# One order of work for five engines, made anew: an adaLN transformer block with sliding-window attention on one core

## The chip, the cores and the metric

The kernel runs on one core of a Trainium2 chip. The core has a matrix engine (TensorE, PE in the profile; its weight loads are listed as PEld), three engines for elementwise work (VectorE or DVE, ScalarE or ACT, GpSimd or POOL), and SyncE (SP), which here does nothing but issue transfers. Each engine runs its own list of instructions in order and waits on semaphores for the others. Sixteen DMA engines move the data of all queues. The metric is the device time of one execution in microseconds (us); a lower time is better.

## What is computed

One input `x` of 2048 rows and 640 columns in bf16, six modulation vectors made from a conditioning row `c`, and two sub-blocks with a residual each:

```python
sa, ca, ga, sb, cb, gb = six rows of (silu(c) @ w_mod)
h = layernorm(x) * (1 + ca) + sa
x = x + ga * A(h)          # 32 heads of 20 columns, causal, window of 256 keys, softmax, @ wo
h = layernorm(x) * (1 + cb) + sb
x = x + gb * B(h)          # (sigmoid(h @ w_gate) * (h @ w_up)) @ w_down, hidden 1536
```

## The kernel before

The 2048 rows are cut into eight chunks of 256 rows, numbered 0 to 7 below (two blocks of 128 rows each). Per chunk the work goes through these stages; the name in brackets is the builder's tag, and the line is the one that the profile shows.

- The chunk of `x` is loaded ("x0" to "x7", L521/L524). VectorE takes the statistics (four `bn_stats`, L732; two `bn_aggr`, L734), GpSimd makes the inverse deviation (L738, L740), and the normalised rows are written (L753 on VectorE, L750 on GpSimd).
- They are turned so that columns lie on partitions. Chunks 0 and 1 are turned on TensorE. From chunk 2 on a DMA transpose does it ("atr", L760, `hT<-x`), and five instructions per chunk apply scale and shift afterwards ("amodu", L768/L769, on any of three engines).
- TensorE projects queries, keys and values in halves of 320 columns (L625, `M<-wq,hT` and so on); VectorE or ScalarE copies each half from PSUM (L655/L656, "evqk", "evv"). Queries and keys go to a staging buffer `stg`, of which there are two, and from chunk 1 on four DMA transposes per chunk turn them, one block of queries or keys each ("qkt", L760, `QT<-stg`, `KT<-stg`). The next chunk's projection may write `stg` only when these transposes have landed.
- Attention: a set of eight or sixteen score matmuls fills the one score tile `S` (L626), ScalarE takes the exponential of all of it (L975, 90 times in the kernel), GpSimd masks it (L983/L985). The product with the values (L626, `M<-E,V`) comes once per half of the heads and fills two PSUM banks, which VectorE transposes (L1021) before they are free again; the result is normalised, turned and projected with `wo` (L625), and VectorE adds the residual (L1094).
- The second norm and its DMA transpose ("btr", `h2T<-x`) follow, then the gated MLP (L625, L1138, L1140) and the output.

PSUM has four banks for everything but the scores (`M`), given out one by one.

The order is not found while building. `Prog.op` notes every operation with what it reads and writes. `Prog.schedule` then goes through the list `PLAN`, which has one number per operation: the number divided by five is the operation in the order of its making, the rest says which engine takes it (0 PE, 1 ACT, 2 DVE, 3 POOL, 4 SP). The place in the list is thus the place in that engine's queue. `SLOTS` gives the buffer of each tile in the same order. `emit` (L279) adds a semaphore wait wherever an operation depends on another engine's, on a landing, or on the last users of its buffer; a transfer carries one of 24 semaphores in turn and also waits for the transfer that had it last. Two more rules touch the steps below: a GpSimd operation waits for the latest VectorE operation that is marked `port`, and `x5` may be loaded only when the transpose of chunk 3 (number 1499) has landed, because it takes that chunk's buffer:

```python
raw = src = load_x(p_x0, a, 0.55 if a < 4 else 20 + 0.1 * a, eng=XE, extra=turned[a - 2])
```

A transfer that waits holds up all that stand behind it in SP's queue; an instruction that waits on VectorE, ScalarE or GpSimd holds up its engine.

Of the kernel before, what the change touches and what calls it, by code (L numbers as in the profile page):

```python
# [305 lines left out]
def c_pe(n):  # L306
# [4 lines left out]
    76, 68, 139, 89, 228, 3, 8, 53, 43, 63, 33, 13, 175, 84, 202, 182, 186, 192, 197, 94, 99, 104, 342, 337, 752, 347,  # L311
    205, 210, 215, 230, 220, 732, 327, 322, 109, 28, 48, 114, 363, 368, 124, 377, 332, 425, 235, 240, 245, 250, 435,
    353, 119, 747, 737, 742, 757, 358, 372, 134, 57, 72, 763, 768, 772, 431, 380, 255, 386, 441, 260, 777, 265, 270,
    275, 390, 820, 280, 287, 457, 447, 467, 462, 451, 780, 406, 396, 402, 129, 585, 423, 827, 590, 485, 417, 597, 786,
    411, 1149, 570, 575, 470, 581, 475, 490, 497, 535, 600, 482, 540, 606, 546, 144, 520, 525, 531, 510, 500, 635, 550,
    506, 556, 1152, 517, 640, 790, 620, 646, 1525, 1167, 1157, 1172, 625, 1162, 1177, 797, 632, 700, 705, 1531, 670,
    610, 810, 675, 1439, 38, 617, 682, 711, 1540, 816, 650, 800, 1546, 685, 690, 1457, 807, 657, 1462, 1447, 18, 164,
    1183, 1538, 1188, 696, 1193, 23, 890, 715, 720, 1198, 1467, 1202, 1555, 726, 560, 660, 895, 905, 910, 567, 1442,
    1561, 875, 880, 1595, 666, 901, 154, 294, 149, 1601, 1452, 917, 1553, 1209, 860, 865, 830, 845, 1473, 850, 856,
    1478, 1568, 835, 1610, 887, 959, 1608, 872, 842, 964, 1616, 1216, 954, 1570, 1030, 935, 1212, 1227, 1582, 1577,  # L320
    1233, 1623, 1223, 1483, 1037, 1625, 1587, 1057, 920, 925, 932, 1631, 1492, 940, 970, 1000, 975, 1592, 2635, 946,
    981, 1040, 1005, 1047, 1012, 1638, 1052, 969, 159, 1265, 1270, 2641, 985, 990, 1107, 1277, 1097, 1102, 2655, 996,
    1640, 1647, 1652, 2544, 1420, 1015, 1425, 1020, 2661, 2675, 1235, 1240, 1325, 1488, 2653, 1027, 1431, 2681, 1280,
    1250, 1087, 1657, 1330, 1092, 2695, 1662, 1079, 174, 1074, 314, 1499, 1336, 2701, 2668, 1247, 1285, 1310, 1315,
    1295, 1300, 1667, 1672, 1322, 2715, 1306, 1061, 1255, 1675, 1690, 1680, 2721, 2552, 1262, 2562, 319, 1695, 1405,
    2547, 1687, 1292, 2567, 1702, 169, 1359, 1364, 2735, 1720, 1725, 1705, 1710, 1717, 2557, 2741, 1375, 1410, 2688,
    2755, 1506, 2761, 2713, 2693, 1390, 2673, 2708, 2733, 1395, 1521, 1511, 1501, 2648, 2728, 2753, 2748, 3099, 1069,
    1732, 1369, 2572, 1417, 1402, 2578, 1380, 1742, 1340, 1345, 2583, 1518, 2588, 2598, 1752, 1757, 1737, 1352, 1374,
    2775, 1747, 1386, 2802, 1762, 2781, 2593, 2603, 2768, 2415, 1110, 2340, 2420, 2788, 1768, 1773, 2773, 2815, 3122,
    3117, 2609, 2797, 2427, 2345, 2821, 2355, 1137, 1117, 2793, 3102, 2352, 1777, 2360, 2400, 2495, 2405, 2366, 2835,  # L330
    2510, 2411, 1782, 2632, 2430, 2385, 2500, 2515, 2507, 2390, 304, 299, 2464, 2841, 2626, 2522, 2828, 2855, 2861,
    2397, 2618, 2469, 2853, 2613, 2370, 2435, 2445, 2480, 2450, 1789, 2375, 2622, 2441, 2875, 2457, 2833, 2873, 2848,
    2485, 2479, 1824, 2955, 2881, 2382, 2474, 2970, 2960, 2807, 3107, 2492, 2868, 2910, 1141, 2975, 3127, 2967, 2893,
    2888, 3190, 1120, 2982, 1132, 3196, 2915, 2895, 2525, 2530, 2900, 3112, 2922, 1127, 2907, 2812, 1792, 3210, 2985,
    3237, 1813, 3133, 1796, 2536, 1801, 3208, 3138, 3143, 3153, 3216, 1829, 3019, 309, 3232, 1834, 1084, 4269, 1807,
    3242, 1852, 2990, 1895, 3080, 3085, 2925, 2930, 2996, 3091, 1857, 3247, 1867, 2937, 3845, 3148, 3158, 3851, 1920,
    1925, 1900, 1930, 1905, 1910, 2940, 1915, 1935, 1819, 1940, 3865, 2945, 3257, 3252, 1946, 2952, 1952, 1955, 1960,
    1965, 1980, 1970, 1975, 1985, 1990, 1995, 3260, 2000, 3871, 3885, 3863, 3164, 3858, 1883, 3878, 3223, 2006, 3265,
    3272, 2012, 3035, 3275, 3280, 2040, 2045, 3040, 3047, 3891, 3905, 1837, 2050, 3000, 3005, 2015, 2020, 2055, 3029,
    3903, 3911, 3188, 3918, 3898, 3883, 3012, 2025, 2030, 2035, 2066, 3065, 3070, 3077, 2060, 3925, 3287, 3034, 3290,  # L340
    3024, 5429, 3228, 3923, 3203, 3181, 3931, 2072, 4287, 3295, 2100, 2105, 2075, 2080, 2085, 2110, 3322, 3302, 4292,
    3327, 2115, 2120, 2090, 1842, 1847, 2095, 2126, 2135, 2140, 2145, 2150, 2155, 2132, 1887, 3945, 2186, 3951, 2160,
    2165, 1873, 1863, 1893, 2170, 2175, 4277, 2180, 3967, 3972, 5447, 2192, 3332, 2195, 3050, 3305, 3310, 3985, 3991,
    3055, 2220, 2225, 2230, 2200, 3062, 2205, 2210, 2215, 3958, 3963, 1877, 3317, 2246, 3337, 3342, 3347, 5432, 2315,
    4005, 4011, 3176, 2255, 2260, 2235, 2320, 2240, 5437, 4003, 4025, 2252, 2295, 2300, 2265, 3938, 3168, 2305, 4031,
    3353, 3358, 3943, 3367, 3362, 5452, 2272, 3171, 4045, 2275, 4018, 4023, 2325, 2280, 2285, 4051, 4140, 4272, 4145,
    3977, 4350, 2312, 2292, 3374, 4065, 4070, 5442, 2332, 4282, 4095, 4100, 4043, 3998, 4063, 4038, 4356, 3393, 4058,
    4077, 4152, 4155, 4106, 4125, 4130, 3377, 3397, 3388, 3381, 4370, 4137, 3982, 4297, 4392, 4160, 3400, 3405, 4376,
    4167, 3410, 3425, 3415, 3420, 3451, 4363, 4303, 4308, 4317, 4397, 4402, 4407, 4080, 5005, 4085, 3430, 4170, 4092,
    4250, 4175, 3435, 3440, 4312, 5011, 5025, 4181, 4255, 4205, 3445, 3485, 5031, 4210, 3490, 3495, 5018, 3500, 5045,  # L350
    4262, 4110, 4115, 4122, 5457, 3457, 4216, 5038, 5023, 3460, 3505, 3465, 5051, 3470, 4368, 3475, 3480, 5063, 3511,
    4204, 3545, 5065, 4324, 5071, 3520, 3550, 3525, 3555, 3530, 3535, 3540, 3560, 3565, 3517, 3571, 4417, 4412, 3577,
    5085, 3605, 4346, 5091, 4235, 3580, 3610, 3585, 3590, 3595, 3600, 3631, 5043, 4388, 5058, 4333, 4240, 5078, 4383,
    5083, 3615, 3620, 3625, 4247, 3637, 5463, 5468, 5105, 5127, 4327, 5132, 5103, 5111, 3640, 4343, 5123, 3645, 3650,
    3665, 3670, 4189, 4199, 3655, 3660, 3675, 4435, 3691, 2339, 5145, 3680, 4420, 4450, 4440, 4425, 5151, 5477, 4432,
    4455, 4447, 5165, 5163, 5118, 4338, 5098, 3685, 3697, 3700, 4220, 3705, 4225, 4232, 3725, 3730, 3710, 5171, 5185,
    3715, 5158, 3735, 3720, 3740, 3760, 5191, 4462, 4482, 4194, 4465, 5183, 4487, 5472, 5484, 5203, 5178, 5198, 4470,
    5205, 3751, 5211, 3745, 5255, 3765, 5137, 4492, 4477, 3757, 5315, 5270, 5320, 5510, 4497, 5327, 5260, 4502, 5218,
    4507, 5267, 5223, 5516, 5581, 5491, 3770, 3777, 4513, 3800, 5275, 5528, 5530, 5142, 5281, 5486, 5536, 5557, 4518,
    5552, 4522, 5562, 5285, 3805, 5290, 3810, 5330, 6170, 3817, 5507, 4527, 5497, 5567, 5335, 3780, 3785, 5296, 6176,  # L360
    3790, 4534, 6190, 3820, 3825, 5240, 6196, 3830, 6188, 5548, 5523, 5543, 6183, 6210, 5572, 5577, 3797, 5342, 3837,
    5365, 5380, 5370, 5385, 5245, 5502, 3844, 6216, 6530, 6230, 6236, 4536, 5392, 5300, 5252, 6203, 6223, 6228, 6208,
    5305, 5585, 5312, 5377, 4542, 6535, 5590, 6545, 5597, 6542, 6250, 5225, 5230, 5237, 6550, 6557, 5615, 5620, 4585,
    6243, 6248, 6256, 4558, 4552, 5627, 6270, 4546, 5354, 4560, 4565, 4570, 4590, 4575, 4580, 4595, 4600, 6292, 6297,
    5359, 6276, 4605, 5349, 6310, 4620, 4645, 4611, 6664, 4617, 5364, 5630, 5635, 4625, 6316, 5600, 4650, 4655, 6330,
    4660, 4665, 5605, 4630, 5642, 6302, 5612, 6336, 6263, 6288, 6328, 4635, 4640, 4671, 4705, 4710, 4680, 6350, 4685,
    6356, 4690, 4695, 4700, 4715, 4720, 4725, 6307, 5647, 5662, 4740, 4731, 6343, 6268, 6283, 6323, 6368, 6348, 6363,
# [874 lines left out]
```

## Time and profile before

| | us |
|---|---|
| median of three runs | 334.14 (334.1 to 334.48) |
| the profiled execution | 334.05 |
| span in it, from the first instruction to the last | 332.3 |
| around the span (334.05 - 332.3) | 1.75 |
| TensorE busy | 320.7, 97% of the span |
| ScalarE, VectorE, GpSimd busy | 227.0, 201.8, 183.0 |
| 16 DMA engines: bytes moved | 33.53 MB, 101 GB/s on average |
| mean granted TensorE clock | 0.995 of full speed |

Busy times are sums over the instructions of an engine. A matmul of 320 columns is listed with a mean near 300 ns, but matmuls overlap, and their ends are modelled; what matters on TensorE are the gaps and the granted clock. Below, a "wait" row names the instruction that waited and the one that released it; the chain of waits starts at the last instruction of the kernel and goes back to whatever released each step; rows of the timeline have start, length, engine, line, operation, tiles and count, with the idle time before in brackets; and a row of the windows view gives, for a stretch, the busy time and the number of instructions of PE, PEld, DVE, ACT and POOL, then the granted clock, the DMA engines' busy share (which counts packets under way, also those that stand still) and the rate.

### The profile page before, as it was taken

What the parts mean: (1) busy time and instruction counts of PE and PEld (TensorE: products, weight loads), DVE (VectorE), ACT (ScalarE), POOL (GpSimd) and SP (SyncE); (2) the same over time, 40 slices, a digit from 0 to 9 for tenths busy, and PEclk for the clock granted to TensorE, in tenths of its full rate; (3) what the DMA queues carried; (4) which work ended last, traced back from release to release, by engine and by line L of the source; (5) the groups of instructions that cost most, each with busy time, mean ns of one, the idle gap of its engine ahead of it and who ended that gap; (6) DMA issues with size and microseconds to landing.
All of it is one profiled execution on the core that took longest, in us unless ns stands there. A gap on an engine that the chain in (4) does not pass through costs nothing.

```text
span 332.3 us, 9821 instructions
## 1 busy us (share of the span) xinstructions
PE 320.7 (97%) x4123; PEld 229.0 (69%) x4123; DVE 201.8 (61%) x440; ACT 227.0 (68%) x215; POOL 183.0 (55%) x273
## 2 busy tenths in 40 slices
PE   5999996979999999999999999999999999999997
PEld 2666663547676777666777667776876677888885
DVE  6697985568487646578564762575544653485423
ACT  2499987668759687887887767789795769321220
POOL 5248588548778647766554774728484555401000
PEclk9999999799999999999999999999999999999999
DMA  7998899999921065033810200160270102102011
GB/s 233 370 373 141 221 248 214 202 216 290 166 62 36 8 73 136 3 82 80 121 49 2 38 5 2 41 145 0 73 113 2 41 2 42 41 0 65 17 41 39
DMA packets 64614, 33.53 MB, mean 101 GB/s; under 512 B 49082, under 2 KB 63034, under 8 KB 64570
## 3 DMA queue, kind: packets, MB, share of 16 engines
q1 hardware_dynamic: 63200, 31.27, 42.1%
q10 hardware_dynamic: 1370, 1.64, 1.5%
q8 instruction: 32, 0.52, 0.7%
q14 instruction: 12, 0.10, 0.1%
HBM read 18.35 MB, written 2.62 MB: 63 GB/s over the span
## 4 chain that ended last, share of the span: by engine, by line
PE 87%; DMA 9%; SPq 1%; ACT 1%; DVE 1%; issue 0%; DVEq 0%
PE M L625 73%; PE S L626 8%; PE M L626 6%; DMA hT<-x 3%; DMA QT<-stg 2%; DMA wd<-in_w_mod_dram 2%; DMA x<-in_A_x_dram 2%; SPq L524 1%; ACT E L975 1%; SPq L760 0%; DVE T L1021 0%; ACT hT L768 0%; DVE hT L814 0%; DVE st L732 0%; PE S L625 0%
## 5 line engine op out<-in xcount | busy, mean ns | idle before, releaser
L975 ACT ACTIVATE E<-S 128x2048 bf16<-128x2048 f32 x90 | 168.9, 1877 | 45.0 <-PE S L626 43.4
L985 POOL TENSOR_SCALAR_AFFINE_SELECT E<-E 128x512 bf16<-128x512 bf16 (+1 forms) x84 | 67.1, 809 | 47.2 <-ACT E L975 36.4
L983 POOL TENSOR_SCALAR_AFFINE_SELECT E<-E 128x512 bf16<-128x512 bf16 (+2 forms) x90 | 73.7, 830 | 26.6 <-ACT E L975 16.0
L625 PE MATMUL M<-h2T,wu 128*128 128x256 bf16 x480 | 74.3, 273 | 0.0
L625 PE MATMUL M<-h2T,wg 128*128 128x256 bf16 x480 | 72.9, 273 | 0.0
L625 PE MATMUL M<-wd,hh 128*128 128x320 bf16 (+2 forms) x396 | 60.5, 295 | 0.0
L1140 DVE SCALAR_TENSOR_TENSOR hh<-sig,M 128x512 bf16<-128x512 f32 x48 | 32.5, 680 | 43.7 <-ACT sig L1138 28.7
L625 PEld LDWEIGHTS M<-h2T,wu 128*128 128x128 bf16 x480 | 45.5, 98 | 9.7 <-issue 1.9
L1138 ACT ACTIVATE sig<-M 128x512 f32<-128x512 f32 x48 | 28.5, 596 | 34.7 <-PE M L625 34.5
L625 PEld LDWEIGHTS M<-h2T,wg 128*128 128x128 bf16 x480 | 45.4, 98 | 9.6 <-issue 2.3
L625 PEld LDWEIGHTS M<-wd,hh 128*128 128x128 bf16 x396 | 37.1, 98 | 14.3 <-issue 1.9
L626 PE MATMUL S<-QT,KT 20*128 20x256 bf16 (+1 forms) x960 | 36.0, 245 | 0.3
L625 PE MATMUL M<-wq,hT 128*128 128x320 bf16 x160 | 28.6, 310 | 4.7 <-DVE T L1021 2.4
L656 DVE CAST stg<-M 128x320 bf16<-128x320 f32 x43 | 20.5, 482 | 17.4 <-PE M L625 17.2
L732 DVE BATCH_NORM_STATS2 st<-x 128x6 f32<-128x320 bf16 x64 | 28.6, 478 | 3.2 <-DMA x<-in_A_x_dram 3.1
L625 PE MATMUL M<-wv,hT 128*128 128x320 bf16 x160 | 29.0, 302 | 0.0
L626 PEld LDWEIGHTS S<-QT,KT 20*128 20x128 bf16 x960 | 14.1, 92 | 20.9 <-ACT E L975 10.7
L625 PE MATMUL M<-wk,hT 128*128 128x320 bf16 x160 | 28.3, 300 | 0.1
L1021 DVE STREAM_TRANSPOSE T<-M 128x512 f32<-128x512 f32 x32 | 21.6, 699 | 10.1 <-PE S L626 9.7
L625 PE MATMUL M<-wo,oT 128*128 128x320 bf16 x160 | 27.4, 299 | 0.0
L1159 DVE TENSOR_TENSOR x<-M,x 128x320 bf16<-128x320 f32 (+2 forms) x33 | 15.3, 471 | 19.7 <-PE M L625 19.5
L1094 DVE TENSOR_TENSOR x<-M,x 128x320 bf16<-128x320 f32 x32 | 15.5, 488 | 16.1 <-PE M L625 16.1
(81 smaller groups left out, 299.9 us busy)
## 6 DMA issues: line engine op xcount, KB each, us to landing
x<-in_A_x_dram SPq DMA_DIRECT2D x10, 320.0 KB, 4.3
wd<-in_w_mod_dram SPq DMA_DIRECT2D x6, 320.0 KB, 5.6
wd<-in_B_w_down_dram SPq DMA_DIRECT2D x4, 480.0 KB, 5.8
out_dram<-x SPq DMA_DIRECT2D x4, 320.0 KB, 2.8
wg<-in_B_w_gate_dram SPq DMA_DIRECT2D x2, 576.0 KB, 8.1
wu<-in_B_w_up_dram SPq DMA_DIRECT2D x2, 576.0 KB, 6.0
wu<-in_w_mod_dram SPq DMA_DIRECT2D x1, 960.0 KB, 12.7
out_dram<-x ACTq DMA_DIRECT2D x3, 320.0 KB, 2.3
```

The source lines that it names most:

```text
L625: return e.matmul(o, l, r, start=st, stop=sp, skip_group_check=True)
L626: return e.matmul(o, l, r, start=st, stop=sp, tile_position=tp, skip_group_check=True)
L656: return e.tensor_copy(dst(), src())
L732: A("dve", lambda e, g, bi=bi, j=j: e.bn_stats(v(bi * 12 + j * 6, 6), src[bi].ap[:, j * 320:(j + 1) * 320]), 0.48, reads=[src[bi].r()], wr ...
L975: A("act", lambda e, eng: e.activation(E.ap[:], Sp.ap[:], ACT.Exp, scale=SM_SCALE), 1.876, reads=[Sp.r()], writes=[E.r()], prio=3, tag=f"e ...
L983: return e.affine_select(ap, ap, pattern=[[0, ap.shape[1]], [1, 128]], compare_op=ALU.is_ge, fill=0.0, base=0, channel_multiplier=-1)
L985: return e.affine_select(ap, ap, pattern=[[0, ap.shape[1]], [-1, 128]], compare_op=ALU.is_ge, fill=0.0, base=-1, channel_multiplier=1)
L1021: A("dve", lambda e, g, h=h: e.transpose(T1.ap[:, 512 * h:512 * h + 512], X[h].ap), 0.694, reads=[X[h].r()], writes=[T1.r(h)], prio=3.5, t ...
L1094: A("dve", lambda e, g, ps=ps, bi=bi, half=half: e.tensor_tensor(x1[bi].ap[:, half * 320:half * 320 + 320], ps.ap[:, 0:320], x1[bi].ap[:, ...
L1138: A("act", lambda e, g, pg=pg, sg=sg: e.activation(sg.ap[:], pg.ap[:], ACT.Tanh, scale=0.5), c_act(512), reads=[pg.r()], writes=[sg.r()], ...
L1140: A("dve", lambda e, g, pu=pu, sg=sg, f0=f0: e.scalar_tensor_tensor(out=hh.ap[:, f0:f0 + 2, :], in0=sg.ap[:].rearrange("p (a b) -> p a b", ...
L1159: A("dve", lambda e, g, ps=ps, bi=bi, c0=c0, n=n: e.tensor_tensor(x1[bi].ap[:, c0:c0 + n], ps.ap[:, 0:n], x1[bi].ap[:, c0:c0 + n], op=ALU. ...
```

## The change

The diff replaces the two constants `PLAN` and `SLOTS` and nothing else. The new list holds the same 1978 operations, so every matmul, elementwise instruction and transfer is still there; what differs is the order on each engine, the buffer that a tile gets, and the engine of those operations that may run on several. According to its author the order was found by a search under fourteen random courses of stopped transfers.

```diff
 PLAN = [
-    76, 68, 139, 89, 228, 3, 8, 53, 43, 63, 33, 13, 175, 84, 202, 182, 186, 192, 197, 94, 99, 104, 342, 337, 752, 347,
...
-    9807, 9875, 9814, 9882, 9889,
+    76, 139, 89, 63, 84, 202, 94, 3, 8, 228, 38, 175, 230, 72, 182, 186, 192, 197, 99, 53, 58, 13, 33, 18, 48, 104,
...
+    9875, 9882, 9889,
 ]
 SLOTS = (
-    "01001001210301320010213210103120231020725310030310201310401301105031206201007032302001312023000013620201213200"
...
+    "01000102123001213000121321010322013202034201071033201000430101110531006210000730320011302023000002602012301110"
...
 )
```

Counted from the two lists: ScalarE takes 232 operations instead of 220 (issues of transfers included), VectorE 422 instead of 440, GpSimd 267 instead of 261; TensorE has 965 and SP 92 in both. SP's queue is the same up to the load of `wv`. From there to the end of chunk 3's transposes it reads as follows (the number in `PLAN`, what it moves, KB for the loads):

| place | before | after |
|---|---|---|
| 1 | 1439 x3 320 | 154 w_mod 640 |
| 2 | 164 wo 480 | 1439 x3 320 |
| 3 | 154 w_mod 640 | 149 w_mod 960 |
| 4 | 294 w_gate 576 | 169 w_mod 480 |
| 5 | 149 w_mod 960 | **1209 hT of chunk 2** |
| 6 | **1209 hT of chunk 2** | 164 wo 480 |
| 7-10 | **959, 964, 954, 969 QT/KT of chunk 1** | **959, 964, 954, 969 QT/KT of chunk 1** |
| 11 | 159 wo 320 | 159 wo 320 |
| 12 | 2544 x4 320 | 2544 x4 320 |
| 13 | 1079 w_up 576 | 299 w_gate 384 |
| 14 | 174 w_mod 320 | **1499 hT of chunk 3** |
| 15 | 1074 w_up 384 | 319 w_mod 320 |
| 16 | 314 w_mod 480 | 314 w_mod 480 |
| 17 | **1499 hT of chunk 3** | 3099 x5 320 |
| 18 | 319 w_mod 320 | 174 w_mod 320 |
| 19 | 169 w_mod 480 | 1074 w_up 384 |
| 20-21 | **1359, 1364 QT of chunk 2** | **1359, 1364 QT of chunk 2** |
| 22-23 | 3099 x5 320, 1069 w_up 576 | **1369, 1374 KT of chunk 2** |
| 24-25 | **1369, 1374 KT of chunk 2** | 294 w_gate 576, **2609 hT of chunk 4** |
| 26-27 | **2609 hT of chunk 4**, 304 w_gate 576 | **2464, 2469 QT of chunk 3** |
| 28 | 299 w_gate 384 | 1069 w_up 576 |
| 29-30 | **2464, 2469 QT of chunk 3** | **1789 h2T of chunk 0**, **2474 KT of chunk 3** |
| 31-32 | **1789 h2T of chunk 0**, **2479 KT of chunk 3** | **2479 KT of chunk 3**, 1829 w_down 480 |

On VectorE the statistics of chunk 5, which need `x5`, stood as two `bn_stats` (3122, 3117) between the two PSUM transposes (2802 and 2797) that follow chunk 1's first product with the values, and two more soon after. In the new list one `bn_stats` (3107) stands ahead of the first of these transposes, one (3102) and a `bn_aggr` (3112) between the two, and the other two (3117, 3122) come behind the copies of chunk 3's projections.

On GpSimd one of the five "amodu" of chunk 3 (1518) moved to ScalarE, and the inverse deviation of chunk 0's second norm (1768) moved ahead of the normalised rows of chunk 4 (2593, 2603) that the transpose 2609 waits for.

More of the change, by code (lines that the diff above doesn't have):

```diff
@@ L310 @@
 PLAN = [
[103 rows of a table removed]
[103 rows of a table added]
 ]
 SLOTS = (
-    "01001001210301320010213210103120231020725310030310201310401301105031206201007032302001312023000013620201213200"
-    "31100040112050314063020027001013000020010013120300213000331120104032300052000103015000210111301021037210303100"
-    "63010220102711000230010201002300310020041311123005003101020031201233021201030010062300007032010013011020202310"
-    "30112032041300500002001000001230210412603131060320007300001103201003202010110320304032011102510031200000011001"
-    "32002120301310623100270012100300113202000331104030005200003001012100131202002030130206200702101000113010210201"
-    "03302110430021005300110002001203020300313106321000700320110030020101023103201030002000112310012010311203001121"
-    "12112030211001302031012012"
+    "01000102123001213000121321010322013202034201071033201000430101110531006210000730320011302023000002602012301110"
+    "03312001043105302112060027000101300020012001303205102003032110104301200052000134001000310121111003100223031231"
+    "20600201102700703200000001120302103010112020432005210300011020300123010220033010210630007032100103000110113020"
+    "02032102304230050021010000013101002310203316306200300070110002030111020213030113004021010102510000300210100103"
+    "02013203131200610050270000310120100010223003101041000251010200001231001130223032200632000730010000001320100201"
+    "11303201042030052100001001011021023121003120106100270023010000001101321020302010000200112301013210312100012130"
+    "20312102310211311201130212"
 )
```

202 rows, old and new, of the table PLAN are left out of this document.

## The prediction

> **What bounds the kernel now.** I began with the busy times, then TensorE's waits, then the chain of waits, and went from each wait to the timeline of the engine behind it.
>
> ```profile
> span 332.3 us, 9821 instructions
> PE 320.7 (97%) x4123; PEld 229.0 (69%) x4123; DVE 201.8 (61%) x440; ACT 227.0 (68%) x215; POOL 183.0 (55%) x273
> ...
> PE 87%; DMA 9%; SPq 1%; ACT 1%; DVE 1%; issue 0%; DVEq 0%
> ```
>
> TensorE sets the time: 97% busy and 87% of the chain. No order removes a matmul, so an order can win only what TensorE loses in waits and in clock. The waits of TensorE, all of them:
>
> ```profile
> PE M L594 <- DMA c_row<-in_c_dram: 2.9, 1, 2.9
> PE M L625 <- DVE T L1021: 2.4, 1, 2.4
> PE M L625 <- DMA QT<-stg: 2.0, 1, 2.0
> PE M L626 <- POOL st L738: 0.6, 1, 0.6
> PE M L625 <- DVE x L753: 0.5, 1, 0.5
> PE M L625 <- DVE hT L814: 0.3, 1, 0.3
> ```
>
> The 2.9, 0.5 and 0.3 lie in the first 12 us, where both lists issue the same transfers in the same order. The other three lie between 50 and 70 us:
>
> ```profile
> 50.82 1.50 PE L626 MATMUL M<-E,V 128*32 128x256 bf16 x64 [0.59 <-POOL st L738]
> ...
> 57.97 1.98 PE L625 MATMUL M<-wq,hT 128*128 128x320 bf16 x7 [2.41 <-DVE T L1021]
> ...
> 69.22 1.79 PE L625 MATMUL M<-wq,hT 128*128 128x320 bf16 x12 [2.03 <-DMA QT<-stg]
> ```
>
> That is 0.59 + 2.41 + 2.03 = 5.03 us. The windows over this place show a fourth loss, in the clock, and how full the other engines are:
>
> ```profile
> 42.00:46.00 4.00, 3.89 (x48) 2.29 (x47) 3.41 (x9) 3.40 (x5) 3.36 (x6) 1.00 1.30 222
> 46.00:50.00 4.00, 4.00 (x36) 2.55 (x34) 3.12 (x11) 3.46 (x3) 3.77 (x5) 1.00 1.06 261
> 50.00:54.00 4.00, 3.41 (x118) 2.46 (x117) 2.57 (x8) 3.81 (x6) 3.73 (x9) 1.00 1.11 253
> 54.00:58.00 4.00, 1.57 (x25) 0.69 (x24) 1.59 (x4) 2.46 (x2) 3.37 (x6) 1.00 1.24 170
> 58.00:62.00 4.00, 4.00 (x23) 2.00 (x24) 2.59 (x8) 1.10 (x3) 0.44 (x1) 0.57 1.12 218
> 62.00:66.00 4.00, 4.00 (x36) 2.61 (x35) 1.59 (x5) 3.90 (x3) 3.47 (x5) 1.00 1.41 210
> 66.00:70.00 4.00, 1.97 (x28) 1.05 (x27) 1.98 (x6) 2.43 (x4) 3.19 (x6) 1.00 0.90 186
> ```
>
> From 58 to 62 us the granted clock was 0.57: 4.00 x (1 - 0.57) = 1.72 us of matmul time lost. So the four losses are 6.75 us.
>
> **What stands behind them** is one late transfer after another:
>
> ```profile
> 38.60 9.74 DMA hT<-x
> 48.34 0.02 issue
> 48.36 0.61 ACT hT L768
> 48.97 1.39 SPq L760
> ...
> 50.47 5.91 DMA x<-in_A_x_dram
> ...
> 61.78 7.35 DMA QT<-stg
> ```
>
> The transpose of chunk 3 (1499) took 9.74 us to land. The medians are much lower:
>
> ```profile
> x<-in_A_x_dram SPq DMA_DIRECT2D x10, 320.0 KB, 4.3
> ...
> QT<-stg SPq DMA_TRANSPOSE x14, 4.5
> KT<-stg SPq DMA_TRANSPOSE x14, 3.5
> h2T<-x SPq DMA_TRANSPOSE x8, 3.4
> ```
>
> When it landed, ScalarE's scale-and-shift, which stood ahead of an exponential in its queue, could run; the next product with the values came 0.59 us late. Then `x5` (3099) could be issued, 5.91 us more, and VectorE stood still:
>
> ```profile
> 56.41 0.89 DVE L732 BATCH_NORM_STATS2 st<-x 128x6 f32<-128x320 bf16 x2 [2.89 <-DMA x<-in_A_x_dram]
> 57.21 0.70 DVE L1021 STREAM_TRANSPOSE T<-M 128x512 f32<-128x512 f32 x1
> ```
>
> The statistics of chunk 5 are not urgent, but the transpose behind them frees a PSUM bank that TensorE wants: that is the 2.41. The third wait is direct: the queries' transpose 2469 landed after 7.35 us, and `stg` was not free. In between, the DMA engines stand still with packets under way:
>
> ```profile
> 44.50:46.00 1.50, 1.50 (x26) 0.90 (x25) 1.50 (x5) 0.90 (x2) 1.50 (x4) 1.00 1.22 32
> ...
> 55.70:57.40 1.70, 0.00 (x0) 0.00 (x0) 0.99 (x3) 1.27 (x1) 1.70 (x3) 1.00 0.40 29
> ...
> 65.30:66.80 1.50, 1.50 (x26) 0.90 (x25) 0.83 (x3) 1.23 (x3) 1.35 (x3) 1.00 0.37 26
> ```
>
> Rates of 26 to 32 GB/s against 170 to 261 in the windows around them: three stops, the first within the landing of 1499, the second at the end of that of `x5`, the third within that of 2469. What starts one no view tells; an order can only keep urgent work out of the way.
>
> **The change, part by part.** *Transpose 1499 and load x5.* Ahead of 1499, after the transposes of chunk 1, stood 2400 KB of loads (320 + 320 + 576 + 320 + 384 + 480); now 1024 KB (320 + 320 + 384). At 261 GB/s, the rate of the window at 46 to 50 us, the difference of 1.41 MB is 5.4 us; issued near 38 us, it should land near 42 instead of 48.34. `x5` now stands behind it and 800 KB of w_mod, and no longer behind two of chunk 2's transposes. At 5.91 us again it is there by about 48. The statistics that need it come no earlier than the product with the values at 50.82. So the waits of 0.59 and 2.41 and the clock loss go: 4.72 us, unless a stop costs more than some 3 us here. At 9.74 again 1499 would land near 48 and `x5` near 54, three us behind that product, and about half of the 4.72 would be back; that end I keep for the range.
>
> *Transposes 2464 and 2469.* Before, 960 KB of w_gate were issued just ahead. Now 576 KB are issued earlier, ahead of 2609, and w_up comes behind. TensorE needs `stg` at 69.22 - 6.75 = 62.5. The issue moves from 61.78 to 61.78 - 4.72 = 57.1; VectorE's new order (a copy of these queries behind two normalised rows of chunk 0) may add half a microsecond. At the median of 4.5 it lands at 62.1, at the 3.4 of a quiet queue at 61.0, at 7.35 at 65.0. So the 2.03 becomes something between nothing and 2.5. I take 0.5, near the median.
>
> *Engines that had slack because TensorE stood still.* GpSimd was busy for 3.36 + 3.77 + 3.73 + 3.37 + 0.44 + 3.47 = 18.14 of the 24 us from 42 to 66. Without 4.72 us of loss there are 19.28 left, 94% full; the modulate that goes to ScalarE gives 0.6 back. VectorE has to empty the same banks in less time, with a `bn_stats` of 0.45 (0.89 for two) ahead of each PSUM transpose. Being late here costs TensorE from nothing to about two masks, at
>
> ```profile
> L983 POOL TENSOR_SCALAR_AFFINE_SELECT E<-E 128x512 bf16<-128x512 bf16 (+2 forms) x90 | 73.7, 830 | 26.6 <-ACT E L975 16.0 <-issue 4.0 <-DVE x L753 2.6
> ```
>
> 0.83 each: 0 to 1.7. I take 0.9, the middle, as both engines are nearly full.
>
> *The rest.* The start hangs on w_mod and the first chunk's loads, which keep their places; the first scores come behind a slightly different mix of projections, 0.3 either way. From 75 us to the end TensorE waits for nothing now. The evacuations of PSUM keep their distances from the matmuls within a few tenths in both lists, so I cost this at nothing, covered by the distance that each copy has; if one copy per chunk came late by 0.2, it would be 1.2 us over chunks 2 to 7, and I keep that in the range. ScalarE gets twelve more operations in its queue, most of them copies, but its exponentials leave room: 227.0 of 332.3 us.
>
> The clock loss needs a word. [...] The rows say: 2.03 us of idle cost none (the clock was 1.00 from 66 to 70), 2.41 cost 1.72.
>
> The sum against the profiled execution: 334.05 - 6.75 + 0.5 + 0.9 = **328.7 us**. The median of the runs, 334.14, lies 0.09 above that execution, which I leave out.
>
> **The rivals.** *The stop at the queries' transposes stays.* The three stops may come at a place in the work and not at a place in the queue; then 2469 is hit again and 2.03 stays: 334.05 - 4.72 + 0.9 = 330.2. For it speaks that one of the three lay on this very transfer, and that TensorE's work around it hardly changes; against it, that fewer bytes stand ahead.
>
> *Everything is covered.* No residue at all: 334.05 - 6.75 = 327.3. Against it: GpSimd at 94%.
>
> *No gain.* If the same bytes meet the same stops, each order loses the same in other places: 334.05. [...] Against this rival: 7.35 and 9.74 us beside a median of 3.4 for `h2T`.
>
> *Slower: GpSimd becomes the bound.* The inverse deviation of chunk 0 (1768) now stands ahead of the normalised rows of chunk 4, and waits for all of VectorE's statistics of that norm. Behind it wait, in order, the rows, the masks, transpose 2609 and, in SP's queue, 2464 and 2469. If GpSimd is held until the old instant, TensorE waits for it as long as it now waits for transfers, and two masks more: 334.05 + 1.7 = 335.7. It decides once GpSimd is held by more than 6.75 us. Against it: the windows above leave GpSimd idle for 3.56 us (58 to 62) and under 0.9 in each of the others, so it would have to be held longer than it ever was.
>
> **How the numbers follow.** Forecast 0.50, the stop stays 0.24, all covered 0.12, no gain 0.06, slower 0.08. The range from 326.8 (all covered, the start 0.5 better) to 332.4 (the stop stays, x5 late by half of 4.72) holds 0.82 of this. About 0.2%, 0.67 us, can be told from no change, so faster means below 333.4: 0.50 + 0.24 + 0.12 and a little less for their tails, 0.86; same 0.06; slower 0.08.
>
> **What would show it.** Right: the wait for `DVE T` of 2.4 gone, no stretch with a clock below 1.00 between 50 and 66 us, 1499 landing within 6 us, and VectorE without an idle before chunk 5's statistics. The residue should be a wait of TensorE for `QT<-stg` or for a PSUM bank between 52 and 66 us. Wrong: a new wait of over 2.4 us anywhere, with the clock falling behind it; GpSimd without a gap from 42 to 66 us; or TensorE's waits after 75 us adding up to more than 1 us.

## The result, and the profile after

The changed kernel takes 329.11 us, the median of four runs (329.05 to 329.42), beside 334.31 for the kernel before on the same chip: a ratio of 0.9841, 95% interval 0.9821 to 0.9861. Its profiled execution took 329.05, with a span of 327.1. The ratios here and below leave out executions over 1.5% above the fastest of the same kernel (four of b_six_loads, two of b_fetch), while the medians and ranges count all; that is why one median below stands above what its ratio says.

The head of the page of the changed kernel, and the chain's shares by engine:

```profile
span 327.1 us, 9812 instructions
...
PE 318.7 (97%) x4123; PEld 227.8 (70%) x4123; DVE 196.7 (60%) x422; ACT 231.4 (71%) x227; POOL 183.0 (56%) x279
...
PE 93%; DMA 3%; DVE 1%; ACT 1%; issue 0%; POOL 0%; SPq 0%; DVEq 0%
```

TensorE now holds 93% of the chain instead of 87, transfers 3 instead of 9. All waits of TensorE in this execution:

```profile
PE M L594 <- DMA c_row<-in_c_dram: 2.8, 1, 2.8
PE S L626 <- DMA QT<-stg: 1.3, 1, 1.3
PE M L625 <- DVE x L753: 1.1, 1, 1.1
PE M L625 <- DVE hT L814: 0.3, 1, 0.3
```

The three waits between 50 and 70 us are gone. A new one is there, of scores and not of a projection: 1.3 for queries that a transpose turns. The chain places it:

```profile
28.67 0.33 PE S L626 x8
29.00 1.37 PE M L626 x65
30.37 4.59 DMA QT<-stg
...
35.05 0.40 PE S L626 x8
```

This is transpose 954 of chunk 1, 4.59 us from issue to landing. The windows over the stretch that lost 6.75 us before, with the sum of those from 42 to 70 us:

```profile
46.00:50.00 4.00, 3.96 (x47) 2.18 (x46) 3.81 (x12) 3.96 (x6) 3.66 (x7) 1.00 1.08 237
50.00:54.00 4.00, 3.98 (x88) 2.86 (x87) 3.74 (x12) 3.98 (x6) 3.64 (x8) 1.00 1.18 216
54.00:58.00 4.00, 3.88 (x77) 2.68 (x75) 3.63 (x11) 3.49 (x2) 3.87 (x6) 1.00 0.82 187
58.00:62.00 4.00, 4.00 (x41) 2.14 (x38) 1.68 (x5) 3.52 (x5) 3.29 (x4) 1.00 1.20 146
62.00:66.00 4.00, 4.00 (x49) 2.44 (x47) 3.19 (x9) 3.74 (x5) 2.93 (x6) 1.00 1.16 312
...
sum 28.00, PE 27.82 PEld 17.48 DVE 22.68 ACT 26.20 POOL 22.78; mean PE 3.97 PEld 2.50 DVE 3.24 ACT 3.74 POOL 3.25
```

The first number behind the length is TensorE's busy time: 3.88 to 4.00 of every 4 us, where three windows of before had 3.41, 1.57 and 1.97. The granted clock is 1.00 in all of them. The other three engines are fuller than before (ScalarE 3.98 of 4 from 50 to 54), and TensorE does not wait for them.

Why it does not, SyncE's timeline and the issues of the window from 37 to 48 us show (there the last number is the time from issue to landing):

```profile
39.21 1.25 SPq L760 DMA_TRANSPOSE hT<-x  x1
...
42.58 1.39 SPq L524 DMA_DIRECT2D x<-in_A_x_dram  x1
```

```profile
x<-in_A_x_dram SPq DMA_DIRECT2D x1, 320.0 KB, 5.5
...
hT<-x SPq DMA_TRANSPOSE x1, 3.4
```

Transpose 1499 landed at 39.2 + 3.4 = 42.6, and `x5` could be issued at once; it was there at 42.6 + 5.5, that is 48.0 (from the unrounded figures). So VectorE's timeline has no idle time for it ahead of the two PSUM transposes; the 0.21 is a wait for TensorE:

```profile
53.84 0.72 DVE L1021 STREAM_TRANSPOSE T<-M 128x512 f32<-128x512 f32 x1 [0.21 <-PE S L626]
54.48 0.45 DVE L732 BATCH_NORM_STATS2 st<-x 128x6 f32<-128x320 bf16 x1
54.97 0.21 DVE L734 BATCH_NORM_AGGREGATE st<-st 128x2 f32<-128x12 f32 x1
55.10 0.66 DVE L1021 STREAM_TRANSPOSE T<-M 128x512 f32<-128x512 f32 x1
```

Put together, from rows alone: the four losses of 6.75 are gone; 1.3 came at chunk 1; the wait for `x` (L753) in the start is 1.1 instead of 0.5, the one for `c_row` 2.8 instead of 2.9. That is 334.05 - 6.75 + 1.3 + 0.6 - 0.1 = 329.1, against 329.05 measured; of the span, 332.3 - 4.95 = 327.35, against 327.1. The account closes within 0.3 us; what it does not say is which part of the change brought it.

### The profile page after: what moved, and what is told of

Read it like the earlier page. It is cut to its first block, busy times and chain, and to the rows that moved or that the text cites. A ratio compares the mean times of both kernels' runs of the same rounds, so it can differ in the third digit from the quotient of the medians.

```text
span 327.1 us, 9812 instructions
## 1 busy us (share of the span) xinstructions
PE 318.7 (97%) x4123; PEld 227.8 (70%) x4123; DVE 196.7 (60%) x422; ACT 231.4 (71%) x227; POOL 183.0 (56%) x279
## 4 chain that ended last, share of the span: by engine, by line
PE 93%; DMA 3%; DVE 1%; ACT 1%; issue 0%; POOL 0%; SPq 0%; DVEq 0%
PE M L625 77%; PE S L626 9%; PE M L626 7%; DMA QT<-stg 1%; DMA x<-in_A_x_dram 1%; ACT E L975 1%; DVE st L732 1%; DVE x L753 0%; SPq L524 0%; POOL st L740 0%; ACT QT L655 0%; DVE hT L814 0%; DVE st L734 0%; DVE x L1159 0%; POOL st L738 0%
## 5 line engine op out<-in xcount | busy, mean ns | idle before, releaser
L985 POOL TENSOR_SCALAR_AFFINE_SELECT E<-E 128x512 bf16<-128x512 bf16 (+1 forms) x84 | 65.6, 790 | 36.4 <-ACT E L975 30.7
L1140 DVE SCALAR_TENSOR_TENSOR hh<-sig,M 128x512 bf16<-128x512 f32 x48 | 32.4, 681 | 49.5 <-ACT sig L1138 27.2
L625 PE MATMUL M<-wk,hT 128*128 128x320 bf16 x160 | 29.4, 300 | 0.0
L625 PE MATMUL M<-wq,hT 128*128 128x320 bf16 x160 | 27.6, 300 | 0.3 <-DVE hT L814 0.3
L656 DVE CAST stg<-M 128x320 bf16<-128x320 f32 x33 | 15.7, 483 | 12.5 <-PE M L625 12.4
```

The costliest lines, as they stand in the source:

```text
L625: return e.matmul(o, l, r, start=st, stop=sp, skip_group_check=True)
L656: return e.tensor_copy(dst(), src())
L985: return e.affine_select(ap, ap, pattern=[[0, ap.shape[1]], [-1, 128]], compare_op=ALU.is_ge, fill=0.0, base=-1, channel_multiplier=1)
L1140: A("dve", lambda e, g, pu=pu, sg=sg, f0=f0: e.scalar_tensor_tensor(out=hh.ap[:, f0:f0 + 2, :], in0=sg.ap[:].rearrange("p (a b) -> p a b", ...
```

## Experiments

| label | what it is | median us (range, runs) | ratio to before, 95% interval |
|---|---|---|---|
| b_1499_first | before, four loads behind 1499 | 333.63 (331.86 to 335.47, 10) | 0.9989 [0.9958, 1.002] |
| b_stats_late | before, chunk 5's statistics later | 333.97 (333.43 to 335.95, 10) | 1.0008 [0.9975, 1.0041] |
| b_six_loads | before, four loads and two more moved | 336.2 (332.1 to 340.52, 10) | 1.0013 [0.9966, 1.006] |
| b_sp_new | before, SP's queue of after | 340.59 (340.48 to 341.6, 4) | 1.0185 [1.0139, 1.023] |
| b_sp_new_dve | the same, one more edit | 339.4 (337.76 to 341.08, 4) | 1.0163 [1.0109, 1.0217] |
| a_sp_old | after, SP's queue of before | 334.52 (332.04 to 335.24, 10) | 0.9985 [0.9958, 1.0012] |
| a_1499_last | after, four loads ahead of 1499 | 330.5 (329.83 to 330.73, 4) | 0.9873 [0.983, 0.9916] |
| a_wo_late | after, one load later | 331.0 (330.05 to 331.8, 10) | 0.9907 [0.9877, 0.9938] |
| a_same | after, unaltered | 328.71 (328.25 to 329.47, 4) | 0.9845 [0.9803, 0.9886] |
| a_wo_early | after, that load earlier | 329.21 (329.07 to 330.26, 4) | 0.9868 [0.9819, 0.9917] |
| a_again | after, finer warm-up | 329.15 (328.72 to 329.73, 4) | 0.9837 [0.9794, 0.988] |
| b_fetch | before, finer warm-up | 334.13 (330.47 to 336.42, 10) | 0.9985 [0.9944, 1.0027] |

The kernel before, run beside these, took from 331.02 to 336.22 us in 57 runs. The diffs below show the queue of one engine, as the list `PLAN` sets it, in place of the long lines of that list.

### One part at a time, in the old order

```diff
 # b_1499_first: SP queue of before
 159 2544
-1079 174 1074 314
 1499
+1079 174 1074 314
 319 169
```

> The order of before with four loads (1079, 174, 1074, 314; 1760 KB) moved in SP's queue from ahead of the transpose 1499 to right behind it; no engine's list is touched. Theory: 1499 lands in about 4 us instead of 9.74, x5 in time, the 0.59, 2.41 and 1.72 go, the 2.03 stays: 329.4 us. Rival (a stop comes at its place in the work and holds 1499 or x5 all the same): no gain, 334.1 us. Rival (the engines' new lists carry the gain): at most the 0.59, 333.5 us.

```diff
 # b_stats_late: VectorE queue of before
 2802
-3122 3117
 2797
+3122 3117
```

> The order of before with two instructions moved on VectorE alone: the bn_stats 3122 and 3117 of chunk 5 go behind the PSUM transpose 2797. Theory (late x5 stops VectorE in front of an urgent transpose): the wait of 2.4 and the clock loss of 1.72 go, the 0.59 and the 2.03 stay, 330.0 us. Rival (the gain of the new order comes from its spread of copies over the engines, and VectorE will stand at the next statistics): at most 0.5 gained, 333.6 us.

```diff
 # b_six_loads: b_1499_first, and in the same queue
 2609
-304 299
 2464 2469
+304 299
```

> The same with two more loads (304, 299; 960 KB of w_gate) moved from ahead of the queries' transposes 2464 and 2469 to behind them. Theory: all 6.75 us go, 327.4 us, below the new order's 329.1, which has a wait of 1.3 of its own. Rival (the stop at the queries' transposes stays): 329.4 us. Rival (the engines' lists carry the gain): 333.5 us.

None gained. In b_stats_late TensorE's wait for `DVE T` is gone, as meant. In b_1499_first 1499 landed 4.65 us after its issue (38.80 to 43.45), but `x5` was not in time, against what was expected: in the old queue it stands behind the transposes 1359 and 1364 of chunk 2 all the same. The chain and VectorE's timeline show it:

```profile
51.10 4.29 DMA x<-in_A_x_dram
```

```profile
55.42 0.89 DVE L732 BATCH_NORM_STATS2 st<-x 128x6 f32<-128x320 bf16 x2 [1.95 <-DMA x<-in_A_x_dram]
```

It was issued at 51.10, where the kernel before issued it at 50.47, and VectorE still stood 1.95 us for it. b_six_loads has the same (1.93 us). So these two mend the transpose alone, and none of the three tries an early 1499 together with an early `x5` in the old queue. The largest waits of b_stats_late, with the windows behind them:

```profile
PE M L625 <- DMA QT<-stg: 2.7, 1, 2.7
...
PE M L625 <- DMA KT<-stg: 1.7, 1, 1.7
```

```profile
66.00:70.00 4.00, 2.23 (x11) 1.43 (x12) 0.49 (x1) 0.60 (x2) 3.38 (x5) 0.80 1.17 222
70.00:74.00 4.00, 4.00 (x47) 2.27 (x48) 2.24 (x6) 2.85 (x4) 0.00 (x0) 0.77 0.94 240
```

And in b_1499_first:

```profile
PE M L625 <- DMA QT<-stg: 2.7, 2, 2.3
...
PE M L625 <- DVE T L1021: 1.0, 1, 1.0
```

TensorE came sooner to the queries' transposes of chunk 3 and had to wait longer for them: waits of 2.7 and 2.3 instead of 2.03, and now with a fall of the clock behind them (0.80 and 0.77; in b_1499_first 0.65 from 66 to 70). In b_six_loads, with these transposes relieved too, the wait for `QT<-stg` shrank to 0.5 and others took its place (`DVE Dr` 1.9, `DVE V` 1.6, `DVE T` 1.0). In each of these three profiles a loss that was lessened was followed by another behind it.

### The queue of transfers without the lists of the engines, and the reverse

In a_sp_old all engines keep their lists and buffers of after, and SP's queue is that of before up to 2474; in b_sp_new it is the other way round, with the whole of SP's queue of after.

```diff
 # a_sp_old: SP queue of after
-154 1439 149 169 1209 164 959 964 954 969 159 2544 299 1499 319 314 3099 174 1074 1359 ...
+1439 164 154 294 149 1209 959 964 954 969 159 2544 1079 174 1074 314 1499 319 169 1359 ...
```

> The changed kernel's lists and buffers on TensorE, VectorE, ScalarE and GpSimd, with SyncE's queue of the kernel before up to chunk 3's last key transpose. If the order of the transfers carries the gain: 1499 lands at 46 us or later, x5 at 52 or later, VectorE waits for x5 ahead of the PSUM transpose again, and the time is 333 to 335. If the order on the engines carries it: within 1 us of 329.1; since the wait of 1.3 at chunk 1's transposes should go as well, 328 to 329.

The chain of a_sp_old:

```profile
48.59 0.46 ACT hT L768
49.05 1.57 SPq L760
...
50.74 5.52 DMA x<-in_A_x_dram
...
56.29 0.49 DVE st L732
56.78 0.40 DVE V L656
...
57.23 0.71 PE M L625 x2
```

and its windows behind the wait:

```profile
54.00:58.00 4.00, 0.77 (x6) 0.22 (x10) 1.71 (x4) 0.80 (x1) 2.98 (x5) 0.83 1.19 180
58.00:62.00 4.00, 4.00 (x64) 2.68 (x65) 2.72 (x9) 1.88 (x1) 0.00 (x0) 0.50 1.06 228
62.00:66.00 4.00, 4.00 (x30) 2.22 (x28) 1.58 (x4) 2.19 (x2) 2.14 (x2) 0.82 1.15 225
```

That is the old story again, link by link: 1499 lands 9.72 us after its issue, ScalarE's scale-and-shift runs at 48.59, `x5` is issued at 50.74 behind chunk 2's transposes, VectorE stands at chunk 5's statistics with a copy behind them that TensorE wants. TensorE waits 3.6, longer than the 2.4 of before (these lists put one of the statistics ahead of both PSUM transposes, and VectorE stands 4.36 us for `x5` instead of 2.89), and the clock falls to 0.50. The whole gain is gone: 334.52.

> The kernel before with its lists and buffers on TensorE, VectorE, ScalarE and GpSimd as they are, and SyncE's whole queue in the changed kernel's order. If the order of the transfers carries the gain: 1499 lands near 42 us, x5 near 48, the waits of 0.59 and 2.41 and the clock loss go, 1.3 comes at chunk 1's transposes: 334.1 - 4.7 + 1.3 = 330.7, or 328.7 if the 2.03 at the queries' transposes goes too. If the lists of the engines are needed as well: 333 to 335, with the loss at another wait between 50 and 80 us.

The queue alone costs 6 us. 1499 lands at 44.02, `x5` at 47.82, no wait for `x5` is left, as the first theory wanted; the loss is elsewhere. The chain:

```profile
85.16 4.80 DMA wd<-in_B_w_down_dram
89.96 0.07 issue
90.04 1.40 POOL wd L1121
91.43 1.18 POOL E L983 x2
```

GpSimd's timeline, and TensorE's:

```profile
90.04 1.40 POOL L1121 TENSOR_TENSOR wd<-wd,gbc 128x640 bf16<-128x640 bf16 x1 [7.59 <-DMA wd<-in_B_w_down_dram]
```

```profile
98.97 2.75 PE L626 MATMUL M<-E,V 128*32 128x256 bf16 x64 [5.10 <-POOL E L983]
```

The new queue issues this piece of `w_down` (1834) at 85.16, right behind the transpose of chunk 5 (3164) and one of chunk 4's queries (3019); the old queue had it in memory at 81.46. GpSimd's old list has the product that needs it ahead of the masks, so GpSimd stands for 7.59 us and TensorE for 5.10. A second loss of the same kind lies at 61 us, where VectorE stands 3.09 us at chunk 4's scale and shift for transpose 2609. That one was moved:

```diff
 # b_sp_new_dve: VectorE queue of b_sp_new
-1782 2632 2507 2522 2397 2622
+1782 2507 2522 2397 2632 2622
```

> b_sp_new (old lists on the engines, new queue of transfers) with one instruction of VectorE moved: the scale and shift of chunk 4 (2632), at which VectorE stood 3.09 us for the transpose 2609, now comes behind two copies of chunk 3's values and one of its queries. If a single list that does not fit the new queue makes that loss: the wait of 5.1 on GpSimd's mask, the 2.1 on VectorE's copy behind it and the clock of 0.57 go, 340.6 - 5 to 8 = 333 to 336. If the old lists fail as a whole: the loss moves to the next place and the time stays above 338.

VectorE's wait for 2609 shrank to 1.14 us, but the median went down by some 1 us only; GpSimd's wait for `w_down` is 8.09 and TensorE's 5.59. So the second theory holds: the old lists fail at several places, and the one edit tried here does not mend them. Neither half of the change is worth anything alone: 0.9985 for the lists with the old queue, whose interval holds 1; 1.0185 for the queue with the old lists; 0.9841 together. Which of the engines' lists the new queue needs, or whether it needs the new buffers, no run takes apart.

### The bytes ahead of 1499, in the new order

```diff
 # a_1499_last: SP queue of after
-2544 299 1499 319 314 3099 174 1074 1359
+2544 1079 174 1074 314 1499 299 319 3099 1359
```

> The changed kernel, with the loads 1079, 174, 1074 and 314 moved ahead of the transpose 1499 and 299 behind it, so that 2400 KB stand ahead of it, as in the kernel before, and x5 behind it. If the bytes ahead of 1499 set its landing: it lands at 46 to 48 us and x5 at 51 to 54, VectorE waits for x5 ahead of a PSUM transpose, the clock falls: 332 to 334. If the new lists on the engines have room for that: below 330.

With 2400 KB ahead 1499 again landed 9.49 us after its issue (38.15 to 47.65), and `x5` at 50.85. The prediction's arithmetic of bytes holds, but the price is 1.4 us (330.5, beside 329.15 for a_again on the same chip) and not 3 to 5, and `x5` isn't in it. One wait of TensorE is new:

```profile
54.70 1.11 PE L625 MATMUL M<-wq,hT 128*128 128x320 bf16 x7 [1.93 <-ACT E L975]
```

The exponential that the row names ran from 52.83 to 54.71 us, past the start of this matmul, so it did not end the wait. The matmul waited for VectorE, for ScalarE and for a landing, and the last of the three to come was the landing of 1364, one of chunk 2's queries' transposes, at 54.57. The issues of the window from 49.5 to 49.6 us have it:

```profile
QT<-stg SPq DMA_TRANSPOSE x1, 5.0
```

Behind the late 1499 in SP's queue it was issued at 49.54 (47.61 in the changed kernel), a stop from 53.0 to 54.4 us fell into it, and it landed at 54.57 (51.80). `x5` is early enough here because it still stands ahead of 1359 and 1364: its landing took 3.2 us. So this run brings back the late 1499 and not the chain from it to `x5`. That chain came back in a_sp_old, where `x5` stands behind these two transposes again.

### The new wait at chunk 1

The load 164 (`wo`, 480 KB) now stands ahead of chunk 1's transposes, and the prediction had given it no price. First it was put behind them:

```diff
 # a_wo_late: SP queue of after
-1209 164 959 964 954 969 159
+1209 959 964 954 969 164 159
```

> The new order with one load moved: w_o (164, 480 KB) goes behind the four transposes of chunk 1 (959, 964, 954, 969) in SP's queue instead of ahead of them. Theory (bytes ahead of a transpose make it late): TensorE's wait of 1.3 for QT<-stg at 33 us goes, 327.8 us. Rival (the stop at that place is what made it late, and it stays): the wait stays near 1.3, 329.1 us.

Both theories missed the time. The wait of 1.3 is gone, as the first had it; in its place VectorE stands at the product of `wo` with its gate, ahead of a PSUM transpose:

```profile
38.26 0.49 DVE L1187 TENSOR_TENSOR wo<-wo,gbc 128x640 bf16<-128x640 bf16 x1 [2.56 <-DMA wo<-in_A_wo_dram]
```

TensorE waits 2.0 for that. The profiled execution took 330.27; five of the ten lie between 330.05 and 330.39 and five between 331.61 and 331.80, of which none was profiled. So `wo` can't come late either, and the next run put it early, beside the changed kernel once more:

```diff
 # a_wo_early: SP queue of after
-154 1439 149 169 1209 164 959
+154 1439 164 149 169 1209 959
```

> The changed kernel once more, unaltered, as the measure for the next run on the same chip: 329.1. Its profile says whether the wait of 1.3 at chunk 1's transposes is there in every execution (then it is the order's) or comes and goes with the stop at 32.7 us, as its absence with the same transfers ahead in a_1499_last suggests.

> The changed kernel with the load 164 (wo, 480 KB) issued right behind 1439 instead of between the transpose of chunk 2 and those of chunk 1. If these bytes ahead of the transposes cause the wait of 1.3: 954 lands 3.1 to 3.6 us after its issue, wo is there far before VectorE wants it, and the time is 327.8. If the w_mod loads that now land some 1.3 us later are what the start waits for, or the wait was a stop's alone: 328.8 to 330.

All waits of TensorE in a_same, an execution of the very same kernel:

```profile
PE M L594 <- DMA c_row<-in_c_dram: 2.3, 1, 2.3
PE M L625 <- DVE x L753: 1.5, 1, 1.5
PE M L625 <- DVE hT L814: 0.2, 1, 0.2
```

No wait at chunk 1, and yet the same span, 327.2. These five executions, two of them of the changed kernel itself, share one list of TensorE, so the start of the same instruction can be compared (us from the span's start):

```
                            after  a_same  a_wo_early  a_1499_last  a_sp_old
a score of chunk 0          23.65   25.09       24.12        23.96     24.10
the last before the wait    31.18   32.62       31.65        31.50     31.64
a score of chunk 1          39.90   39.95       39.34        38.83     38.97
another                     60.67   60.72       60.33        61.45     66.21
one of chunk 2              72.34   72.39       72.00        73.11     78.28
the last projection        324.39  324.44      324.41       325.16    330.31
```

The execution a_same came 1.44 us later to chunk 1 and found the transposes done; that of `after` came early and waited. In `after` 954 took 4.6 us and held a standstill of its packets (32.7 to 34.3 us, below); in a_same it took 3.5, in a_1499_last, with the same queue ahead, 3.1. So the wait took a stop that met this transpose and an execution that came early to it; the 480 KB alone do not bring it. The early `wo` (954 in 3.1) was ahead by 0.34 us until 72 and had lost it at the end; its time, 329.21, cannot be told from a_same's. No version here beats the changed kernel.

### Where the stops come from

No view shows what starts a stop, but the trace holds every packet. One queue on the page of after carries instructions (packets, MB, share):

```profile
q8 instruction: 32, 0.52, 0.7%
```

These are 32 packets of 16 KB for 8246 records of TensorE (4123 matmuls and as many weight loads), one per 258. A stop is taken here as eight or more of the transposes' 256-byte packets that stand for over 1 us together. To see whether the two belong together, TensorE's instruction stream was shifted while all real work stayed as it is:

```diff
-            for k in range(n):
-                ins = e.matmul(p_S.aps[0][:, 3, :], Eall[:, 0, 0:128], Eall[:, 0, 128:640], start=True, stop=True)
+            for k in range(4 * n):
+                ins = e.matmul(p_S.aps[0][:, 3, 0:128], Eall[:, 0, 0:128], Eall[:, 0, 128:256], start=True, stop=True)
```

> The changed order, with the warm-up matmuls at the start cut into four times as many of a quarter of the columns: the same matmul time, but 96 more instructions in TensorE's stream ahead of all real work. The raw packets show a fetch of instructions on queue q8 about every 258 TensorE instructions, and a standstill of the transposes' packets behind many of them. If the fetches set the stops, fetches and stops come 96/258 of an interval of some 10 us, about 3.5 us, earlier in the work than in the changed kernel (there at 48.5, 54.0 and 60.7 us), and the waits of TensorE fall on other transfers: 328.5 to 331. If the stops belong to the transfers themselves or to an instant, they stay within 1 us of those places, and the time stays at 329.1.

From the raw packets, starts in us up to 120:

```
after    fetches  17.6  24.7  32.4  42.0  53.3  60.4  71.9  80.2  90.4  97.0  108.6  118.0
         stops    25.3  32.7  48.5  60.7  74.6  82.0  118.2
a_again  fetches  13.9  23.5  32.4  40.6  53.5  57.3  67.8  77.7  88.7  94.2  105.3  113.8
         stops    32.6  41.1  48.7  53.8  57.9  68.2  82.4  90.2  114.1
```

The trace of a_again has 90 more records of TensorE (8336), where the expectation counted 96 instructions, and fetches that moved by up to 4.2 us, not by an even 3.5. The stop of 60.7 came at 57.9 and that of 118.2 at 114.1, with their fetches; that of 32.7 stayed, as did its fetch; 48.5 and 82.0 stayed within 0.4 us, with no fetch just ahead. The stop at 54.0 us that the expectation names for the changed kernel is none by this count. Over all 14 profiles, 79 of 110 stops begin within 1 us after a fetch has begun, though fetches are some 10 us apart; for the other 31 the cause stays open. The time did not change: 329.15. Under these shifted stops the new order lost no more. The old one was put to the same test, with the same edit:

> The kernel before with the warm-up cut as in a_again: 96 more TensorE instructions ahead of all work, so that the instruction fetches and the stops behind them come some 3.5 us earlier in the work. If the loss of the old order comes from the bytes ahead of 1499 and from the order of VectorE and of the queue, it stays: 333 to 336, with 1499 landing 8 us or more after its issue. If it was a chance meeting of three stops with three transfers: 329 to 331.

It keeps its loss, at 334.13, with 1499 landing 8.11 us after its issue and a fall of the clock to 0.57, now behind another wait:

```profile
PE M L625 <- POOL st L738: 2.2, 1, 2.2
PE M L625 <- DVE h2T L769: 1.7, 1, 1.7
```

So the loss of the old order was not a chance meeting of three stops with three transfers: under another course the same loss comes at other places. It does not come in every execution, though: three of b_fetch's ten kept the clock at 1.00 (330.47, 331.21 and 332.3), and so did five of the 57 of the kernel before (331.02 to 333.93).

## Why the prediction was right, point by point

**The four losses (6.75).** All gone, in the manner predicted for the first three: 1499 landed at 42.6 ("near 42"), `x5` at 48.0 ("by about 48"), the clock stayed at 1.00. That the loads ahead of 1499 set its landing is shown: 9.49 us with them moved ahead (a_1499_last), 3.35 without (after). Over all 14 profiles it is 8.1 to 9.7 us in the five with 2400 KB ahead, in either order, and 3.4 to 5.2 in the nine with 640 to 1504 KB. That "one late transfer after another" lost the time is shown for the new lists: a_sp_old rebuilt the whole chain and lost the whole gain. In the old lists an early 1499 and an early `x5` were not enough: b_sp_new had both (44.02 and 47.82), had no wait for `x5`, and lost more elsewhere. The gain needs queue and lists together. The prediction read the four losses as one row of causes in the old order, and did not see that their removal there lets others appear; its rival of no gain, "each order loses the same in other places", describes what the single edits to the old order did.

**The queries' transposes (0.5 taken).** Nothing was left. The forecast put the issue of 2469 at 57.1, its landing at 62.1 and TensorE's need at 62.5. It was issued at 58.94 and landed at 63.22, after 4.28 us, with a stop inside (60.7 to 62.1); the first instruction of TensorE that waits for it came at 63.61. All three lie 1.1 to 1.8 us behind the forecast, about as much as the start was longer, and the landing came 0.4 us ahead of the need, as forecast; the 0.5 was a reserve that was not used. The rival's premise, that stops come at a place in the work, is borne out in part by the fetches (79 of the 110 stops begin within 1 us after one has begun); its conclusion, that 2469 would be late by 2.03 again, is not.

**Full engines (0.9 taken).** From 42 to 70 us TensorE was busy for 27.82 of 28 us, so 0.18 at most. GpSimd had 3.66, 3.64, 3.87 and 3.29 of 4 from 46 to 62, that is 90% where the forecast had 94%, and cost nothing.

**The start (0.3 either way).** This term was mis-sized: 0.6 more at `x`, 0.1 less at `c_row`, and 1.3 at transpose 954, together +1.8. The load of `wo` had been moved past four transposes and was not costed. In the event it took a stop, and another execution paid nearly the same in a later start. The 1.4 that the sum took for the queries' transposes and the full engines did not come; this 1.8 came in its place. That 328.7 lies so near 329.05 is therefore luck: the place of the residue, "between 52 and 66 us", was wrong, and its size fitted by chance.

**After 75 us (nothing).** No wait there in the profile after.

**The slower rival.** GpSimd did not become the bound with 1768 where it is now. b_sp_new shows its mechanism at another place: an instruction of GpSimd ahead of the masks that waits for a transfer, 7.59 us, of which TensorE feels 5.10. The price taken for it, 1.7, was too low for such a case.

## What to carry to other kernels

An order for several engines and a queue of transfers is one object: to carry over its queue alone cost 1.9%, its lists alone brought nothing, and the single edits to the old order that were tried brought nothing either, since another wait stood close behind each. Judge an order by what it does under several courses of delays and not by one trace: the old order ran from 331 to 336 us in 57 executions, the new one from 328.3 to 329.5 in eight, and from 328.7 to 329.7 with the stops shifted. And cost every transfer that a moved load passes, on its own line, even where the trace of before has no wait.

## What the runs showed of the hardware

**Fetches of instructions and transposes.** Of 123 fetches of 16 KB during which eight or more of the transposes' packets were under way, 80 met a stop. Of the 110 stops 89 took 1.2 to 1.8 us; the longest took 2.7. What a fetch costs TensorE's own stream no run here isolates.

**The clock.** A window row gives a mean. Cut at the right instants, the windows of the kernel before show what lies behind the 0.57:

```profile
54.70:58.00 3.30, 0.89 (x20) 0.42 (x21) 1.59 (x4) 1.88 (x1) 2.73 (x5) 1.00 1.30 135
58.10:61.40 3.30, 3.30 (x17) 1.65 (x18) 2.46 (x8) 0.53 (x2) 0.00 (x0) 0.50 1.11 205
```

The trace's own record of the clock has it at 0.50 from 58.08 to 61.49 us and at 1.00 around that. In all profiles a fall (those in the last microsecond left aside) is to 0.50 and lasts 3.41 us, or 6.83 (a_sp_old, and one each in b_sp_new and b_sp_new_dve), so, worked out from these lengths, it costs up to 1.7 or 3.4 us of matmul time. In before the changes of the record stand at 6.88, 58.08 and 61.49 us. The prediction set the 2.03 us of before beside the 2.41 as if length decided. Set side by side, the profiles do not show that. The clock fell behind waits of 2.18 (b_fetch), 2.25 (b_1499_first), 2.41 (before), 2.69 (b_stats_late) and 3.58 us (a_sp_old). In b_six_loads it fell too, to a mean of 0.67 from 74 to 78 us, behind 1.80 us of idle from 70 to 74 (busy for 2.20 of 4.00), and no wait there after the start was longer than 1.9. It stayed at 1.00 behind the 2.03 of before and the 1.93 of a_1499_last. What decides whether the clock falls behind some 2 us of idle no run here isolates.
